# Cached attention: V in 2 KB rows, P times V as pairs of 64-row tiles, and a new order of the engines' work

## The chip, the cores and the metric

One core of a Trainium2 chip runs the whole kernel. The time is that of the device, in microseconds (us); medians of several runs are quoted. The engines are PE (matrix multiplies; PEld is its weight load), DVE (VectorE), ACT (ScalarE), POOL (GpSimd) and SP (SyncE, which only issues loads here). A run counts as slow when it is over 1.5% above the fastest run of the same kernel.

## The reference

Two independent blocks A and B, each a cached attention layer; bf16 throughout.

```python
# x (16, 64, 640), k_cache and v_cache (16, 32 heads, 512 keys, 128), wq (640, 4096), wo (4096, 640)
q = (x @ wq).reshape(B, Sq, H, Dh).transpose(0, 2, 1, 3)
scores = einsum("bhqd,bhkd->bhqk", q, k_cache) * Dh ** -0.5
p = softmax(scores, axis=-1)
o = einsum("bhqk,bhkd->bhqd", p, v_cache)
out = o.transpose(0, 2, 1, 3).reshape(B, Sq, H * Dh) @ wo
# result: concatenate([A, B], axis=-1)
```

K and V are 268 of the 292 MB that are read. Each pair of caches is used once.

## The kernel before

The work is cut into 128 packs: a pack is two batch elements and four heads. `build_plan` gives every operation a time in slots (a slot is about the time of one pack); sorting by it fixes each engine's order, and semaphores are derived from the reads and writes. SP's order of loads comes from deadlines. K and V have rings of five packs (buffers that are used in turn).

```python
AT = dict(..., QP=-1 + 0.40, QE=-1 + 0.58, KT=(-1 + 0.08, -1 + 0.70), S=0.0, ...
          TR=(0.95, 1.28), TE=(1.02, 1.38), PV=(1.20, 1.60), OE=(1.50, 1.72), OP=(1.70, 1.86), ...)

def em_LDV(e, op):                       # V: a head's 512 keys over 128 partitions, 4 keys = 1 KB each
    ...
    src = blocks[blk][2][2 * bp + b, 4 * j:4 * j + 4].rearrange("g (p t) d -> p g t d", p=128)
    ins = e.dma_start(v_ring[:, n % NV, b], src)

def em_S(e, op):                         # scores: 32 matmuls on 32-row, 64-column tiles
    ...
def em_TR(e, op):                        # 8 transposes for two heads; twice a pack
    ...
def em_PV(e, op):                        # P times V, twice a pack
    m = op.idx
    n, a = m // 2, m % 2
    for s in range(2):
        for b in range(2):
            for t in range(4):
                col = s * 128 + 64 * b
                last = e.matmul(o_ps[:, col:col + 64], v_ring[:, n % NV, b, 2 * a + s, t, :],
                                pT_ring[:, m % NT, s, t, 64 * b:64 * b + 64], start=(t == 0), stop=(t == 3))
...
def em_OP(e, op):                        # output projection: 512 + 128 columns a head
    ...
```

A matmul in the program is two PE instructions, LDWEIGHTS and MATMUL. So a pack costs PE 2 x (32 S + 16 transposes + 20 Q projection + 32 P times V + 8 output projection) = 216 instructions.

## Time and profile before

824.84 us, median of 3 runs (823.98 to 826.99).

| what | before |
|---|---|
| DMA | 376 GB/s in nearly every slice; 131,072 V packets of 1 KB, median 47 ns; 32,768 K packets of 4 KB, median 161 ns |
| PE, one pack without a stop | 5.31 us |
| PE, mean of packs 2 to 127 | 6.00 us |
| first pack after the start-up | 49.8 us; after the last S 18.6 us |

The first lines are the page's rows of 40 equal slices of the span: the busy share of PE and of the DMA engines in tenths, then GB/s.

```profile
PE   3069999999999999998778989999999999999994
...
DMA  9999999999999999999999999999999999999980
GB/s 329 364 372 367 377 378 376 378 373 379 373 374 376 371 380 375 373 375 370 339 319 377 372 378 377 376 376 376 376 375 373 377 373 376 375 374 376 377 284 13
```

Both PE and DMA look full. The next lines are the DMA queues: packets, MB, and the share of the 16 engines' span.

```profile
q1 hardware_dynamic: 193280, 292.06, 100.2%
q8 instruction: 112, 1.84, 0.9%
```

q1 carries the data (its packets overlap in time, hence over 100%). q8 carries instructions: 112 packets of 16,384 bytes for PE's 27,682 instructions, 1.84 MB, or 66 bytes each. PE's program is fetched block by block while the kernel runs, by the DMA engines that also bring K and V.

Now one pack on PE, in order of time: start, length, engine and line, operation, count.

```profile
331.10 1.14 PE L403 MATMUL ps<-kt_ring,qs_ring 32*64 32x512 bf16 x32
332.16 0.64 PE L462 MATMUL ps<-pT_ring,v_ring 128*128 128x64 bf16 x16
332.64 0.61 PE L446 MATMUL ps<-ident,pn_ring 128*128 128x128 bf16 x8
333.09 1.28 PE L380 MATMUL ps<-xT_ring,wqp_sb 128*128 128x128 bf16 x20
334.20 0.63 PE L462 MATMUL ps<-pT_ring,v_ring 128*128 128x64 bf16 x16
...
336.40 0.44 PE L403 MATMUL ps<-kt_ring,qs_ring 32*64 32x512 bf16 x8
```

S (L403) to S takes 336.40 - 331.10 = 5.30 us with no idle time between the groups (the left out lines are the output projection and the second transposes). (Lengths overlap: the profile models a matmul's end. Only starts are used here, so 332.16 to 332.64 is P times V.) Over the kernel the medians from each group's first weight load to the next group's are S 1.07, P times V 0.45 and 0.49, transposes 0.43 and 0.59, Q projection 1.12, output projection 1.17 us: some 5.31 us, which is called a pack without a stop below. But the mean pack takes 6.00. The group of P times V (busy us, mean ns | idle before it, releaser) and the table of waits (total us, times, longest) show what is between:

```profile
L462 PE MATMUL ps<-pT_ring,v_ring 128*128 128x64 bf16 x4096 | 168.6, 194 | 21.8 <-issue 11.4
```

```profile
PE ps L403 <- issue: 13.4, 21, 1.3
...
PE ps L462 <- issue: 11.4, 23, 1.9
...
PE ps L462 <- DMA v_ring<-in_B_v_cache_dram: 7.9, 11, 1.8
DVE kt_ring L393 <- DMA kn_ring<-in_A_k_cache_dram: 7.5, 1, 7.5
```

"issue" means that PE waited for nothing that the profile shows. Data is hardly ever late: 7.9 us on V, 7.5 us on K, once. SP instead waits for free K slots:

```profile
SPq L342 <- DVE kt_ring L393: 187.2, 123, 3.8
```

### The profile page before, as it was taken

To read this page: it belongs to the slowest core of one execution; us is meant where nothing else is said; L and a number is where in the kernel's file an instruction comes from. 1 tells how busy PE (TensorE), PEld (TensorE's weight loads), DVE (VectorE), ACT (ScalarE), POOL (GpSimd) and SP (SyncE) were. 2 spreads that over 40 slices of the span, in tenths; PEclk is the share of its full clock that TensorE was granted. 3 is DMA by queue.
4 is the path that set the end of the run, shared out by engine and by line. 5 is a ranking of instruction groups with operands and counts; after the bars stand their busy time and mean duration, and the time that the engine had idled before them with its cause. 6 is when DMAs were issued, how large, how long until landed. Compare 5 with 4: busy or idle time off the path is not lost.

```text
span 824.6 us, 31476 instructions
## 1 busy us (share of the span) xinstructions
PE 707.0 (86%) x13777; PEld 521.7 (63%) x13905; DVE 578.7 (70%) x902; ACT 419.6 (51%) x1313; POOL 388.2 (47%) x550
## 2 busy tenths in 40 slices
PE   3069999999999999998778989999999999999994
PEld 2046776767666767676556666666666666666773
DVE  3047787777777787777556767777777777787773
ACT  2025655555554645554444555555555464555552
POOL 2068444444444444445665444444454444454442
PEclk9999999999999999999999999999999999999997
DMA  9999999999999999999999999999999999999980
GB/s 329 364 372 367 377 378 376 378 373 379 373 374 376 371 380 375 373 375 370 339 319 377 372 378 377 376 376 376 376 375 373 377 373 376 375 374 376 377 284 13
DMA packets 195729, 296.79 MB, mean 360 GB/s; under 512 B 9216, under 2 KB 162816, under 8 KB 195584
## 3 DMA queue, kind: packets, MB, share of 16 engines
q1 hardware_dynamic: 193280, 292.06, 100.2%
q8 instruction: 112, 1.84, 0.9%
q10 hardware_dynamic: 2304, 2.62, 0.9%
q14 instruction: 33, 0.27, 0.1%
HBM read 292.03 MB, written 2.62 MB: 357 GB/s over the span
## 4 chain that ended last, share of the span: by engine, by line
PE 70%; DMA 10%; SPq 6%; issue 6%; POOL 5%; DVE 3%; ACT 0%; ACTq 0%
PE ps L380 15%; PE ps L403 14%; PE ps L462 14%; PE ps L446 12%; PE ps L476 9%; DMA v_ring<-in_B_v_cache_dram 8%; PE ps L479 5%; DMA ws_ring<-in_A_wq_dram 2%; SPq L349 2%; SPq L342 2%; DVE kt_ring L393 2%; POOL pn_ring L438 2%; POOL wqp_sb L356 1%; POOL wqp_sb L357 1%; SPq L335 1%
## 5 line engine op out<-in xcount | busy, mean ns | idle before, releaser
L438 POOL TENSOR_SCALAR pn_ring<-p_ring,recip 128x512 bf16<-128x512 bf16 x512 | 349.2, 694 | 382.0 <-DVE recip L433 382.0
L418 ACT ACTIVATE p_ring<-ps 128x512 bf16<-128x512 f32 x512 | 304.2, 597 | 262.2 <-PE ps L403 262.2
L393 DVE STREAM_TRANSPOSE kt_ring<-kn_ring 128x1024 f32<-128x1024 f32 x256 | 316.0, 1235 | 7.6 <-DMA kn_ring<-in_A_k_cache_dram 7.5
L451 DVE COPY pT_ring<-ps 128x1024 bf16<-128x1024 bf16 x256 | 177.1, 692 | 161.3 <-PE ps L446 161.3
L446 PE MATMUL ps<-ident,pn_ring 128*128 128x128 bf16 x2048 | 158.0, 220 | 48.0 <-POOL pn_ring L438 46.8
L462 PEld LDWEIGHTS ps<-pT_ring,v_ring 128*128 128x128 bf16 x4096 | 141.5, 98 | 80.1 <-issue 64.7
L462 PE MATMUL ps<-pT_ring,v_ring 128*128 128x64 bf16 x4096 | 168.6, 194 | 21.8 <-issue 11.4
L380 PE MATMUL ps<-xT_ring,wqp_sb 128*128 128x128 bf16 x2560 | 169.7, 222 | 11.4 <-issue 9.1
L403 PE MATMUL ps<-kt_ring,qs_ring 32*64 32x512 bf16 x4096 | 155.2, 398 | 15.5 <-issue 13.4
L446 PEld LDWEIGHTS ps<-ident,pn_ring 128*128 128x128 bf16 x2048 | 122.4, 98 | 64.3 <-POOL pn_ring L438 49.1
L380 PEld LDWEIGHTS ps<-xT_ring,wqp_sb 128*128 128x128 bf16 x2560 | 153.1, 114 | 14.7 <-issue 11.4
L468 ACT ACTIVATE oT_ring<-ps 128x256 bf16<-128x256 f32 x256 | 98.5, 385 | 117.6 <-PE ps L462 117.4
L476 PE MATMUL ps<-wo_sb,oT_ring 128*128 128x512 bf16 x384 | 132.9, 387 | 0.1
L386 DVE TENSOR_SCALAR qs_ring<-ps 128x512 bf16<-128x512 f32 x128 | 88.6, 692 | 60.7 <-PE ps L380 60.7
L479 PE MATMUL ps<-wo_sb,oT_ring 128*128 128x128 bf16 x512 | 113.0, 221 | 8.2 <-issue 1.7
L418 ACT ACTIVATION_READ_ACCUMULATOR p_ring<-ps 128x1 f32 x512 | 105.6, 206 | 0.0
L403 PEld LDWEIGHTS ps<-kt_ring,qs_ring 32*64 32x64 bf16 x4096 | 57.1, 104 | 63.1 <-issue 24.4
L476 PEld LDWEIGHTS ps<-wo_sb,oT_ring 128*128 128x128 bf16 x512 | 50.3, 98 | 65.6 <-ACT oT_ring L468 33.3
L479 PEld LDWEIGHTS ps<-wo_sb,oT_ring 128*128 128x128 bf16 x512 | 50.7, 99 | 0.2 <-issue 0.2
L433 DVE RECIPROCAL recip<-rowsum 128x2 f32<-128x2 f32 x256 | 36.3, 142 | 6.6 <-ACT p_ring L418 6.4
L356 POOL COPY wqp_sb<-ws_ring 128x1280 bf16<-128x1280 bf16 x16 | 20.0, 1253 | 41.4 <-DMA ws_ring<-in_A_wq_dram 41.4
L357 POOL COPY wqp_sb<-ws_ring 128x1280 bf16<-128x1280 bf16 x16 | 20.1, 1256 | 0.0
(19 smaller groups left out, 39.5 us busy)
## 6 DMA issues: line engine op xcount, KB each, us to landing
kn_ring<-in_A_k_cache_dram SPq DMA_DIRECT2D x128, 512.0 KB, 10.2
v_ring<-in_A_v_cache_dram SPq DMA_DIRECT2D x128, 512.0 KB, 10.7
kn_ring<-in_B_k_cache_dram SPq DMA_DIRECT2D x128, 512.0 KB, 10.2
v_ring<-in_B_v_cache_dram SPq DMA_DIRECT2D x128, 512.0 KB, 10.7
ws_ring<-in_A_wq_dram SPq DMA_DIRECT2D x8, 640.0 KB, 9.4
wo_sb<-in_A_wo_dram SPq DMA_DIRECT2D x8, 640.0 KB, 10.6
ws_ring<-in_B_wq_dram SPq DMA_DIRECT2D x8, 640.0 KB, 8.3
wo_sb<-in_B_wo_dram SPq DMA_DIRECT2D x8, 640.0 KB, 11.2
```

Source lines behind the costliest of these rows:

```text
L380: last = e.matmul(ps[:, 0, f * 128:(f + 1) * 128], w[:, kt, f, :], xT_ring[:, xs, kt, :], start=(kt == 0), stop=(kt == KT - 1))
L386: ins = e.tensor_scalar(qs_ring[:, op.idx % NQ].rearrange("p f b q -> p (f b q)"), ps[:, 0, :], scale, None, ALU.mult)
L393: ins = e.transpose(dst, kn_ring[:, n % NK, b, :].bitcast(F32))
L403: last = e.matmul(ps[64 * b:64 * b + 64, i, :], qs_ring[rows, n % NQ, f, b, :], kt_ring[rows, n % NKT, b, :, f // 2, :, f % 2], start=(f = ...
L418: ins = e.activation(dst, src, ACTF.Exp, scale=1.0, accum_out=rowsum[:, h:h + 1])
L438: ins = e.tensor_scalar(pn_ring[:, h % NPN, :], p_ring[:, h % NP, :], recip[:, (h // 2) % NR, h % 2:h % 2 + 1], 1.0, ALU.mult, ALU.mult)
L446: last = e.transpose(pt_ps[:, s, t, :], pn_ring[:, h % NPN, t * 128:(t + 1) * 128], ident[:, :])
L451: ins = e.tensor_copy(pT_ring[:, op.idx % NT].rearrange("p s t q -> p (s t q)"), pt_flat)
L462: last = e.matmul(o_ps[:, col:col + 64], v_ring[:, n % NV, b, 2 * a + s, t, :], pT_ring[:, m % NT, s, t, 64 * b:64 * b + 64], start=(t == ...
L468: ins = e.activation(oT_ring[:, op.idx % NO].rearrange("p s q -> p (s q)"), o_ps, ACTF.Copy)
L476: last = e.matmul(out_ps0, oT_ring[:, m % NO, s, :], wo_sb[:, h, 0:N0], start=(h == 0), stop=(h == H - 1))
L479: last = e.matmul(out_ps1, oT_ring[:, m % NO, s, :], wo_sb[:, h, N0:D], start=(h == 0), stop=(h == H - 1))
```

## The change

The intent: the DMA engines look saturated, and V's 1 KB rows cost more per byte than K's 4 KB rows. With 2 KB rows a head's 512 keys fill only 64 partitions, so two heads share the 128; P times V must then contract over 64 rows, in pairs of tiles. The two tiles of a pair write different banks of PSUM, the memory that PE writes its results to; one of these is shared with the last 128 output columns, which are therefore added up in SBUF by DVE once a pack (`OA`). P times V, its eviction and the output projection run once a pack instead of twice, and the order on all engines is new.

```diff
-    AT = dict(XT=-2 + 0.90, XE=-2 + 0.93, QP=-1 + 0.40, QE=-1 + 0.58, KT=(-1 + 0.08, -1 + 0.70), S=0.0,
-              ...
-              TR=(0.95, 1.28), TE=(1.02, 1.38), PV=(1.20, 1.60), OE=(1.50, 1.72), OP=(1.70, 1.86),
+    AT = dict(XT=-0.988, XE=-0.9, QP=-0.582, QE=-0.071, KT=(-0.704, -0.567), S=0.0,
+              ...
+              TR=(0.869, 1.222), TE=(1.062, 1.39), PV=1.623, OE=1.67, OP=2.225, OA=2.403,
 ...
-            src = blocks[blk][2][2 * bp + b, 4 * j:4 * j + 4].rearrange("g (p t) d -> p g t d", p=128)
+            src = blocks[blk][2][2 * bp + b, 4 * j:4 * j + 4].rearrange("(a s) (p t) d -> (s p) a (t d)", s=2, t=8)
 ...
-                    for t in range(4):
-                        col = s * 128 + 64 * b
-                        last = e.matmul(o_ps[:, col:col + 64], v_ring[:, n % NV, b, 2 * a + s, t, :],
-                                        pT_ring[:, m % NT, s, t, 64 * b:64 * b + 64], start=(t == 0), stop=(t == 3))
+                    for t in range(8):
+                        for s in range(2):
+                            rows = slice(64 * s, 64 * s + 64)
+                            col = a * 128 + 64 * b
+                            last = e.matmul(o_ps[:, s, col:col + 64], v_ring[rows, n % NV, b, a, t, :],
+                                            pT_ring[rows, (2 * n + a) % NT, t, 64 * b:64 * b + 64],
+                                            start=(t == 0), stop=(t == 7), tile_position=(64 * s, 0))
 ...
+        def em_OA(e, op):
+            j = op.idx % NJ
+            dst = out_sb[:, N0:D] if j == NJ - 1 else acc[:, :]
+            ins = e.tensor_copy(dst, out_ps1) if j == 0 else e.tensor_tensor(dst, acc[:, :], out_ps1, ALU.add)
 ...  (rings of P and P^T laid out by 64 keys and two heads; PSUM banks moved; a constant tile dropped)
```

P times V is now 64 matmuls a pack instead of 32: 280 PE instructions instead of 216.

## The prediction

> **What bounds the kernel now.** Two things nearly tie. The page's slice rows show the DMA engines busy in 9 tenths or more of every slice but the last two (376 GB/s). Yet compute hardly waits for data: the table of waits gives PE 7.9 us on V, VectorE 7.5 us on K. K lies landed 10 to 15 us before its transpose in the first half, 1.6 to 8.6 us in the second. In the steady state PE sets the pace. The timeline from 331.09 to 336.40 us is one pack with PE back to back: S 1.07, P times V 0.45 and 0.49, transposes 0.43 and 0.59, Q projection 1.11, output projection 1.17: 5.31 us. Packs average 5.9. The missing 0.6 us is holes in PE's stream that the waits call "issue". From 60 to 800 us I count 72 (75 us), nearly all ending 2.5 us after a 16 KB packet of the "instruction" queue (112 packets, 1.84 MB, for PE's 27,682 instructions: 66 B each). PE outruns its instruction fetch. Whole time: first real pack at 49 us, 126 packs at 6.0 us average (the block change costs some 15 us extra), 18 us of tail.
>
> **What the change does.**
> - DMA: V's 131,072 packets of 1 KB (median 46 ns, 4 KB ones 161 ns) become 65,536 of 2 KB; by the straight line between those, estimated 84 ns each instead of 92. Saves about 35 us of 16-engine time: some 785 us of DMA at full rate become 750. Off the steady critical path; it can remove at most the 15 us at the block change. The Trainium skill ("DMA: Bandwidth & Descriptors", Why small descriptors are slow) gives a fixed cost per packet; the trace agrees, about 8 ns.
> - PE: 32 P-times-V matmuls a pack (29 ns start to start) become 64 on 64 rows. The Trainium skill ("TensorE: Matmul & The Clock Gate", Part 3) says that matmuls on different row groups run concurrently; S does so in this trace. So I estimate 30 to 45 ns a pair: 1.0 to 1.4 us instead of 0.94. Two more changes of tiling mode, 0.1 us each (the breaks around S), add 0.2. PE without holes: estimated 5.5 to 5.9 us.
> - Fetch: 276 PE instructions a pack instead of 212, 64 of the new ones in the fastest stretch. With 2.5 us from fetch to use and about 75 instructions in hand (both from the trace), estimated holes grow from 0.6 to about 0.9 us a pack.
> - VectorE gains one 128x128 addition a pack (estimated 0.25 us on its 4.8). ScalarE's evictions shrink. Neither binds. P times V waits for that addition; Q projection covers it mostly.
> - Startup: PE still idles from 17 to 49 us behind the third Wq load, which the static order still puts after some 27 loads.
>
> **Time.** Pack estimated 6.2 to 6.9 us, mostly 6.5: 49 + 126 x 6.5 + 18 = 885 us. Range 825 to 945. Chances: faster by over 2% 0.10, within 2% 0.13, slower by over 2% 0.77.
>
> **What would show it.** Mean V packet near 84 ns, the queue's wait for K slots growing from 187 us; "instruction" packets near 144; PE holes over 100 us; P-times-V pair pitch 30 to 45 ns; K ready ever longer before use.
>
> **What would make it wrong.** Fetch holes that shrink once DMA is less loaded; a startup that the new order mends; pairs that don't overlap (pitch 60 ns: above 945 us); or DMA binding more than I think, which would give about 790 us.

(The counts in it, 212 and 276, leave out four instructions; they are 216 and 280. The same slip is in the expectations and names of the experiments below: 244 stands for 248, 228 for 232.)

## The result

893.87 us median of 4 runs (882.31 to 899.52), against 825.72 us for the kernel before. The ratio is 1.0745, with a 95% interval of 1.0639 to 1.0851. Ratios here are the mean time of one kernel's fast runs over that of the other's in the same rounds, so not quite the ratio of the medians. Two of the four runs count as slow by the 1.5% rule; the profiled one (span 894.0 us) is one of them, the fast ones are 882.31 and 891.87, and the granted clock does not tell them apart (0.977 and 0.984 in the slow ones, 0.981 and 0.988 in the fast). The reading below therefore leans on what the experiments show too.

The slices after:

```profile
PE   3078789888997897997978878888988989889885
...
DMA  9999989999998999899999998899998989989830
GB/s 341 378 379 390 374 320 362 335 319 376 326 368 311 364 382 344 314 367 303 331 385 389 391 396 317 288 361 312 362 346 267 388 299 367 338 302 360 311 124 13
```

DMA is no longer full (330 GB/s over the span, from 357), so the change has not made loads the limit. The queues:

```profile
q1 hardware_dynamic: 127744, 292.06, 90.2%
q8 instruction: 143, 2.34, 1.0%
```

The median V packet of 2 KB took 84 ns, as estimated, so the loads did become cheaper, though less than the two shares suggest: 90.2% of the longer span is 806 us of all 16 engines, 100.2% of the span before was 826. The instruction packets went from 112 to 143. PE's group of P times V (idle before it 33.2 us, from 21.8), PE's waits, and SP's wait for K slots:

```profile
L465 PE MATMUL ps<-pT_ring,v_ring 64*128 64x64 bf16 x8192 | 148.0, 191 | 33.2 <-issue 32.3
```

```profile
PE ps L465 <- issue: 32.3, 27, 3.8
...
PE ps L405 <- issue: 25.3, 21, 3.1
PE ps L447 <- issue: 18.4, 12, 2.5
...
PE ps L465 <- DVE acc L489: 0.7, 2, 0.4
```

```profile
SPq L344 <- DVE kt_ring L395: 413.9, 214, 5.8
```

The pairs themselves are fast. From the start of P times V to the next group it is 1.04 us for 64 matmuls, 16 ns from start to start where a full-array one took 29, so two run side by side. Before, the two halves took 0.94 us. A pack without a stop is now S 1.07, transposes 0.41, output projection 1.09, Q projection 1.26, P times V 1.04 and transposes 0.55, in this order: 5.42 us, only 0.11 more. The wait over the shared bank ("DVE acc") is 0.7 us in all. What grew are PE's waits on "issue", and SP waits twice as long for K slots because PE is behind. One such stop, in the same columns as the pack above:

```profile
304.03 0.90 PE L465 MATMUL ps<-pT_ring,v_ring 64*128 64x64 bf16 x50
305.80 0.38 PE L465 MATMUL ps<-pT_ring,v_ring 64*128 64x64 bf16 x14 [0.87 <-issue]
306.11 0.62 PE L447 MATMUL ps<-ident,pn_ring 128*128 128x128 bf16 x8
```

PE stops inside P times V, after 50 of 64 matmuls, for 0.87 us. Nothing in the program stands there, neither a semaphore nor a switch of shape. The longest:

```profile
673.75 1.07 PE L465 MATMUL ps<-pT_ring,v_ring 64*128 64x64 bf16 x61
678.57 0.28 PE L465 MATMUL ps<-pT_ring,v_ring 64*128 64x64 bf16 x3 [3.75 <-issue]
```

### What a hole is

I looked for stops of over 0.45 us, from the start of one PE instruction to the start of the next, that ended 1.1 to 1.9 us after an instruction packet had been transferred ("holes"), from 60 us to the last S. Before there are 50 of them, 45.9 us; after 81, 122.1 us. Counting PE's instructions in the trace, semaphore instructions included, they lie at one place in every 256. Most traces lack one matmul of a pack's output projection; with it put back, all 50 holes before lie at the same place, and after 78 of 81, the other three one instruction beside it. In experiment e1 below, whose trace lacks none, 94 of 96 do. 16,384 bytes are 256 instructions of 64 bytes. PE has run to the end of a block and the next is not there.

The Trainium skill ("Runtime: NRT & Kernel Launch", Instruction fetch mechanics) says that instructions come in 16 KiB blocks of 256, which this trace confirms, and that the cost of crossing a block is mostly hidden, which it does not: holes are 122.1 of 894.0 us.

The accounts of the 69.4 us between the two spans: holes +76.2 us; a pack without a stop +0.11 us, times 126 gives +13.9; other stops of over 0.45 us 29.6 before and 3.3 after (before, nearly all at the change of block A to B and in the 150 us after it, where loads were behind), -26.3. That sums to 63.8; the rest, some 6 us, lies in shorter stops, start-up and tail.

### The profile page after: what moved, and what is told of

It reads as the page before. It is cut to its first block, busy times and chain, and to the rows that moved or that the text cites. A ratio compares the mean times of both kernels' runs of the same rounds, so it can differ in the third digit from the quotient of the medians.

```text
span 894.0 us, 39557 instructions
## 1 busy us (share of the span) xinstructions
PE 732.5 (82%) x17873; PEld 541.9 (61%) x18001; DVE 602.4 (67%) x1030; ACT 405.1 (45%) x1185; POOL 386.8 (43%) x550
## 3 DMA queue, kind: packets, MB, share of 16 engines
q1 hardware_dynamic: 127744, 292.06, 90.2%
## 4 chain that ended last, share of the span: by engine, by line
PE 80%; issue 13%; SPq 3%; DMA 1%; ACT 1%; POOL 0%; DVE 0%; ACTq 0%
PE ps L405 17%; PE ps L382 16%; PE ps L447 16%; PE ps L465 15%; PE ps L481 10%; PE ps L483 6%; SPq L351 1%; SPq L344 1%; DMA ws_ring<-in_A_wq_dram 1%; ACT p_ring L420 1%; PE ps L365 1%; SPq L337 0%; POOL pn_ring L440 0%; POOL wqp_sb L358 0%; POOL wqp_sb L359 0%
## 5 line engine op out<-in xcount | busy, mean ns | idle before, releaser
L420 ACT ACTIVATE p_ring<-ps 128x512 bf16<-128x512 f32 x512 | 298.5, 598 | 211.5 <-PE ps L405 211.5
L447 PE MATMUL ps<-ident,pn_ring 128*128 128x128 bf16 x2048 | 164.3, 223 | 49.5 <-POOL pn_ring L440 29.8
L472 ACT ACTIVATE oT_ring<-ps 128x512 bf16<-128x512 f32 x128 | 76.4, 597 | 264.4 <-PE ps L465 264.4
L447 PEld LDWEIGHTS ps<-ident,pn_ring 128*128 128x128 bf16 x2048 | 118.9, 99 | 111.5 <-DVE pT_ring L453 39.8
L405 PE MATMUL ps<-kt_ring,qs_ring 32*64 32x512 bf16 x4096 | 159.2, 406 | 27.4 <-issue 25.3
L465 PE MATMUL ps<-pT_ring,v_ring 64*128 64x64 bf16 x8192 | 148.0, 191 | 33.2 <-issue 32.3
L465 PEld LDWEIGHTS ps<-pT_ring,v_ring 64*128 64x128 bf16 x8192 | 129.3, 95 | 48.5 <-issue 36.4
L481 PE MATMUL ps<-wo_sb,oT_ring 128*128 128x512 bf16 x384 | 123.0, 390 | 6.9 <-issue 6.9
L489 DVE TENSOR_TENSOR acc<-acc,ps 128x128 f32<-128x128 f32 x96 | 27.4, 285 | 29.8 <-PE ps L483 22.0
L358 POOL COPY wqp_sb<-ws_ring 128x1280 bf16<-128x1280 bf16 x16 | 20.0, 1251 | 42.5 <-DMA ws_ring<-in_A_wq_dram 42.5
```

The source lines that it names most:

```text
L405: last = e.matmul(ps[64 * b:64 * b + 64, i, :], qs_ring[rows, n % NQ, f, b, :], kt_ring[rows, n % NKT, b, :, f // 2, :, f % 2], start=(f = ...
L420: ins = e.activation(dst, src, ACTF.Exp, scale=1.0, accum_out=rowsum[:, h:h + 1])
L447: last = e.transpose(pt_ps[:, t, :], pn_ring[:, op.idx % NPN, t].rearrange("q s k -> q (s k)"), ident[:, :])
L465: last = e.matmul(o_ps[:, s, col:col + 64], v_ring[rows, n % NV, b, a, t, :], pT_ring[rows, (2 * n + a) % NT, t, 64 * b:64 * b + 64], star ...
L472: ins = e.activation(oT_ring[:, op.idx % NO].rearrange("p s a q -> p s (a q)"), o_ps, ACTF.Copy)
L481: last = e.matmul(out_ps0, oT, wo_sb[:, h, 0:N0], start=(h == 0), stop=(h == H - 1))
```

## The experiments

The theory: 64 more PE instructions a pack make PE reach the end of a fetched block sooner than the next one comes. Rivals: the new order or the chain over the shared bank costs the time; the 2 KB rows disturb something; the tiles are slow. The kernel before beside them had medians of 826.54 us (e1 to e4), 823.91 (e5 to e8), 824.98 (e9) and 825.28 (e10).

### e1: only the instructions, in the kernel before

```diff
-                    last = e.matmul(ps[:, 0, f * 128:(f + 1) * 128], w[:, kt, f, :], xT_ring[:, xs, kt, :], ...)
+    for hb in range(2):   # the 128 columns in two halves
+                    last = e.matmul(ps[:, 0, c0:c0 + 64], w[:, kt, f, :], xT_ring[:, xs, kt, 64*hb:64*hb + 64], ...)
-                last = e.matmul(out_ps0, oT_ring[:, m % NO, s, :], wo_sb[:, h, 0:N0], ...)
+    for q in range(4):    # the 512 columns in four quarters
+                last = e.matmul(out_ps0[:, c0:c0 + 128], oT_ring[:, m % NO, s, :], wo_sb[:, h, c0:c0 + 128], ...)
```

> The kernel before with 276 PE instructions a pack, as many as the changed kernel has, and the same columns streamed: the Q projection's 128-column matmuls cut in two of 64, the output projection's 512-column ones in four of 128. V rows, order, tiles and PSUM as before; the result is right. Fetch theory: holes after an instruction fetch grow from 0.6 to about 1.1 us a pack, some 138 fetches as in the changed kernel, total 870 to 895 us. Rival (order, shared bank or DMA rows cost the time): only the few ns of streaming more, 825 to 835 us.

933.52 us (928.49 to 939.06), ratio 1.1276, result correct. Nothing but the number and size of PE's instructions changed, and the kernel before became slower than the changed one. A pack without a stop rose from 5.31 to 5.54 us (that is 29 us of the 107), holes from 45.9 to 141.1 us. Slices, queue and waits:

```profile
DMA  9999899999899899997889999989999899899940
...
q8 instruction: 144, 2.36, 1.0%
```

```profile
PE ps L465 <- issue: 35.9, 25, 2.6
...
PE ps L481 <- issue: 25.9, 18, 2.4
```

I had expected 870 to 895: holes came to somewhat more per fetch than in the changed kernel (141.1 us over 139 fetches against 122.1 over 138), and the 64-column halves cost more streaming than I had allowed.

### e2: the changed kernel with half the instructions of P times V

```diff
-                for b in range(2):
-                    ... e.matmul(o_ps[:, s, col:col + 64], v_ring[rows, n % NV, b, a, t, :], pT_ring[..., 64 * b:64 * b + 64], ...)
+                    ... e.matmul(o_ps[:, s, a * 128:a * 128 + 128], v_ring[rows, n % NV, 0, a, t, :], pT_ring[rows, ..., t, :], ...)
```

> The changed kernel with half the P-times-V instructions: one 128-column matmul with one batch element's V in place of two 64-column ones (32 matmuls a pack instead of 64; result wrong on purpose). Columns streamed, tiling mode, order, DMA, PSUM as in the changed kernel. Fetch theory: holes fall from 1.0 to about 0.6 us a pack, 109 or so fetches, total 820 to 840 us. Rival (order, waits, DMA rows, bank): stays at 880 to 895 us.

783.04 us (782.37 to 783.48), ratio 0.9477. The result is wrong (both batch elements use the first one's V); loads, order, tiles, banks and streamed columns are those of the changed kernel, and a pack without a stop takes 5.37 us. Holes: 3.1 us. The slices' GB/s, the instruction queue, and PE's waits at P times V:

```profile
GB/s 331 385 376 383 393 398 397 398 397 399 397 396 399 379 398 391 392 397 396 353 383 387 388 391 398 396 398 396 396 395 393 395 395 393 396 391 393 397 342 28
...
q8 instruction: 111, 1.82, 1.0%
```

```profile
PE ps L463 <- DMA v_ring<-in_B_v_cache_dram: 6.3, 6, 1.8
...
PE ps L463 <- issue: 0.6, 2, 0.3
```

This was better than I had expected. Everything else in the change is good; the 64 extra instructions cost more than 100 us of its time (783.04 against 887.09, the mean of the changed kernel's fast runs). With them gone, DMA is full again, now at 395 GB/s.

### e3: the new order alone

V in 1 KB rows again and P times V as 32 full-array matmuls once a pack, in the changed kernel.

```diff
-            src = ....rearrange("(a s) (p t) d -> (s p) a (t d)", s=2, t=8)
+            src = ....rearrange("g (p t) d -> p g t d", p=128)
-                    for t in range(8):
-                        for s in range(2):  # 64-row tiles
+                    for s in range(2):
+                        for t in range(4):  # 128 rows; the rings of P laid out as before
```

> The changed kernel's order, rings, shared bank and extra VectorE addition, but V in 1 KB rows on 128 partitions and P times V as 32 full-array matmuls a pack (result right). Fetch theory: PE at 5.3 us and holes at 0.6 us a pack, total 815 to 835 us, like the kernel before. Rival (the order or the once-a-pack chain over the shared bank costs the time): 870 us or more.

817.93 us (817.32 to 818.71), ratio 0.9898, result correct. The order and the shared bank cost nothing; a pack without a stop is 5.20 us, holes fall to 23.4 us. Other stops are 43.1 us, one of them of 17.7 us at the block change. From pack 40 on, but for the block change, K lies ready only 1 to 2 us before use, so this kernel is bound by its loads:

```profile
GB/s 329 365 372 367 377 377 377 378 376 376 370 378 375 367 377 371 373 375 371 369 369 371 369 374 378 368 380 374 377 377 362 377 376 363 377 376 376 378 357 47
```

### e4: 2 KB rows alone

The kernel before with the other source pattern for V; V stands in the wrong places, so the result is wrong.

```diff
-            src = ....rearrange("g (p t) d -> p g t d", p=128)
-            ins = e.dma_start(v_ring[:, n % NV, b], src)
+            src = ....rearrange("(a s) (p t) d -> (s p) a (t d)", s=2, t=8)
+            ins = e.dma_start(v_ring[:, n % NV, b].rearrange("p (a e) t d -> p a (e t d)", a=2), src)
```

> The kernel before with V fetched in 2 KB rows and nothing else changed (V stands in the wrong places, result wrong on purpose). Theory (PE bounds the steady state, DMA only the block change): 810 to 825 us. Rival (DMA bounds the whole): 785 to 800 us. If 2 KB rows somehow slow the instruction fetch: above 835 us.

805.90 us (804.49 to 806.34), ratio 0.9747: 20.6 us, between the theory's 1 to 16 and the rival's 25 to 40, so a miss for both. Part is fewer holes (30.6 us against 45.9), part fewer other stops (22.6 against 29.6). So cheaper loads also help PE, which I had not foreseen.

### e5 and e6: the same two kernels with light loads

From the sixth pack on each K and V transfer carries a quarter of its bytes (results wrong). All engines' work stays.

```diff
-            ins = e.dma_start(kn_ring[:, n % NK, b, :], src)
+            w = 2048 if n < NK else 512
+            ins = e.dma_start(kn_ring[:, n % NK, b, 0:w], src[:, 0:w])     # V likewise
```

> The kernel before; from the sixth pack on each K and V transfer carries a quarter of its bytes (1 KB rows; result wrong on purpose). Work of all engines and PE's instructions as before. If the 2.5 us from fetch packet to use and the late fetches are PE's own affair: holes stay at about 0.6 us a pack, only the wait at the block change goes, 800 to 815 us. If instruction fetches come late because they queue behind the data in the DMA rings: holes nearly vanish, 735 to 760 us.

> The changed kernel with the same cut of the K and V bytes (result wrong on purpose). Own affair of PE: stays at 865 to 895 us. Queueing behind data: its PE needs 5.41 us a pack without holes, so 740 to 775 us.

765.61 us (763.21 to 766.28), ratio 0.9289, for the kernel before, and 764.00 us (761.72 to 764.45), ratio 0.9260, for the changed one (the first is 6 us above its range, the second inside). The holes are nearly gone: 4.5 and 7.5 us. The two of the kernel before do not lie at a block's end. The five of the changed one do, and all fall between 371 and 422 us, where the data rate rises from some 110 to 204 to 272 GB/s. Elsewhere PE runs through with 280 instructions a pack. Slices and queue of the changed kernel with light loads, and PE from a P times V on:

```profile
DMA  9996333333334444434679443333333334343300
...
q8 instruction: 143, 2.34, 1.3%
```

```profile
303.77 1.11 PE L467 MATMUL ps<-pT_ring,v_ring 64*128 64x64 bf16 x64
304.81 0.62 PE L449 MATMUL ps<-ident,pn_ring 128*128 128x128 bf16 x8
305.36 1.13 PE L407 MATMUL ps<-kt_ring,qs_ring 32*64 32x512 bf16 x32
```

So PE's instructions do not come late by themselves. They come late because the DMA engines are busy with data. From the moment at which PE executed the last instruction of one block, and so came to the next, to the start of the packet that brings the block after that, the median is 4.7 us in the kernel before and 1.0 us with light loads; in the changed kernel 3.8 and 0.7 us. From the packet's start to PE's next instruction after a hole it is 2.4 to 2.6 us in all kernels. The Trainium skill ("DMA: Bandwidth & Descriptors", Queues, rings and completion order) says that each engine takes turns between its queues, a whole packet at a time, and that such a packet is typically some 9 to 17 descriptors. If a descriptor is what the profile calls a packet, a single row (no run here shows it), one turn of 4 KB rows at 161 ns each is an estimated 1.4 to 2.7 us, from that page's count and this trace's time. So waiting for turns may be a good part of the delay of 4 us, but it is not shown.

### e7: an earlier start of PE

```diff
-    t_now = -8.0
+    t_now = -4.0        # in e3: SP's plan starts later in its own time, so the third Wq load comes sooner
```

> The changed kernel's order with V in 1 KB rows (818 us in the earlier run), and the DMA queue's static plan started later in its own time (-4 slots instead of -8), so that the third Wq load comes after some 11 loads instead of 27 and PE's first idle stretch (17 to 49 us) ends sooner. If DMA bounds that kernel from end to end: 808 to 818 us, little gain. If the late start of PE still counts: 790 to 803 us. Result right.

817.59 us (816.81 to 817.93), ratio 0.9916, result correct. The first pack after the start-up comes at 27.2 us instead of 49.8, and the end does not move. That kernel is bound by its loads from end to end, as e3 said; PE's idle stretch at the start is free.

### e8: a dose between

Wide matmuls as in e2, for one of the two head pairs only: 248 instructions a pack; result wrong.

> The changed kernel with the wide P-times-V matmuls for one of the two head pairs of a pack only: 244 PE instructions a pack, between 212 (783 us) and 276 (890 us); result wrong on purpose. Fetch theory, cost growing with the instructions: 825 to 850 us. If instead the cost comes only past a threshold near 276: 785 to 805 us.

826.81 us (824.17 to 831.55), ratio 1.0018; holes 77.5 us. Between 783 and 894 and at the lower end of what was expected: the cost grows with the count and is not a threshold at 280.

### e9: fewer loads under way

If the fetch queues behind the loads under way, fewer of them should help. A load now also waits until the one four (or three) before it has landed; results are right.

```diff
-            for op in progs[eng]:
+            for i, op in enumerate(progs[eng]):
                 waits = list(op.waits)
+                if eng == "sp" and i >= 4:
+                    old = progs[eng][i - 4]
+                    waits.append((old.sem, old.count))
```

> The changed kernel, complete and right, with one more wait in the load queue: a load is issued only when the load four before it has landed, so at most four are under way (before: issue to landing 10 us at 1.35 us a load, some seven under way). Queueing theory: an instruction fetch then starts 1 to 2.5 us after its block boundary instead of 3.8, holes fall below 0.3 us a pack, DMA stays full; 775 to 805 us. Rival (the fetch is slowed by the sharing of the engines at full rate, not by the depth of the queue): 870 us or more.

> The same with at most three loads under way (about 4 us of data[...]). Queueing theory: fetches start sooner still, but the DMA engines may run dry between loads; 775 to 815 us. Rival: 870 us or more.

> The kernel before with at most four loads under way (right). Queueing theory: its holes (0.6 us a pack) go too, and what is left is DMA with 1 KB rows: 805 to 820 us. Rival: unchanged at 825 us, or slower if four are too few to keep the engines full.

Misses in time, all three. They were run on another chip. The changed kernel with four: 868.80 us (863.53 to 868.96), ratio 1.0520, some 18 us less than its fast runs without (887.09), but far from 805. There the limit changes little: SP waits for free slots anyway, and the median time from issue to landing only fell from 6.5-7.1 us to 5.8-5.9. The median fetch starts 3.98 us after the crossing, against 3.83 without the limit; the delays only vary less (eight in ten lie between 2.5 and 5.1 us, against 1.0 and 5.8), and holes are 100.8 us instead of 122.1. With three: 1013.53 us (1011.09 to 1016.08), ratio 1.2290; the engines run dry (293 GB/s) and PE waits for data, with a delay of 2.9 us and holes of 40.0 us.

The kernel before with four: 868.17 us (865.37 to 872.77), ratio 1.0521, slower than without, at 341 GB/s over the span instead of 360. Here the limit does change the queue: from issue to landing the median fell from 10.2-10.7 us to 6, the fetch's delay from 4.7 to 2.6 us, and the holes from 45.9 to 8.7 us, of which only 0.5 us lie at a block's end. So the holes went, as the queueing theory had said, but PE now waits for V:

```profile
PE ps L462 <- DMA v_ring<-in_B_v_cache_dram: 44.8, 41, 2.4
...
PE ps L462 <- DMA v_ring<-in_A_v_cache_dram: 28.5, 22, 2.3
```

The loads under way are thus part of the delay in the kernel before (or the lower data rate that came with fewer of them; the runs do not separate the two). They do not explain the delay of the changed kernel, and a limit that takes the holes away costs more in data than it gains.

### e10: a trade between the two limits

In e3, every fourth pack gets 2 KB rows and tiled pairs (232 instructions a pack on average).

```diff
+            if n % 4 == 0:
+                ...  # V "(a s) (p t) d -> (s p) a (t d)", 64-row pairs
+            else:
+                ...  # V "g (p t) d -> p g t d", full array
```

A first build, which is not on record, was refused before it ran, for a race: a pack of one layout overwrote P while the half of another layout was still read. One more dependency, which the recorded edit has, mended it.

> A trade between the two limits: the changed kernel's order; every fourth pack has V in 2 KB rows and P times V in pairs of 64-row tiles, the other three have 1 KB rows and full-array matmuls (result right). DMA falls by a quarter of the 2 KB rows' gain (from the 818 us of the all-1-KB kernel by some 9 us); PE instructions are 228 a pack on average, between 212 (hardly a hole) and 244 (827 us). If both limits move as the runs suggest: 800 to 812 us, faster than both kernels. If the pack with 276 instructions pays its holes in full: 818 to 830 us.

821.26 us (818.80 to 823.73), ratio 0.9964, result correct. It was run on another chip. It missed the 800 to 812 us that I hoped for and fell in the range of holes paid in full: loads got cheaper (380 GB/s in many slices), but holes rose to 63.0 us from 23.4.

The best right version stays e3 (or e7): about 1% faster than the kernel before, and 8% faster than the changed one.

### One rule over the runs

Let a block's time be 256 instructions at the pace of a pack without a stop, and the fetch's time be its median delay after the crossing plus the time from its packet to PE's next instruction (2.4 to 2.6 us). The fetch is late by the difference.

| kernel | instructions a pack | block, us | fetch, us | late by | holes per fetch, us | time, us |
|---|---|---|---|---|---|---|
| e5 before, light loads | 216 | 6.29 | 3.5 | -2.8 | 0.04 | 765.61 |
| e6 changed, light loads | 280 | 4.95 | 3.3 | -1.7 | 0.05 | 764.00 |
| e9 before, four under way | 216 | 6.29 | 5.1 | -1.2 | 0.08 | 868.17 |
| e2 changed, wide | 216 | 6.37 | 6.4 | 0.0 | 0.03 | 783.04 |
| e9 changed, three under way | 280 | 4.95 | 5.4 | 0.4 | 0.29 | 1013.53 |
| e3 order alone | 216 | 6.17 | 6.6 | 0.5 | 0.22 | 817.93 |
| e4 2 KB rows alone | 216 | 6.29 | 6.8 | 0.5 | 0.29 | 805.90 |
| before | 216 | 6.29 | 7.2 | 0.9 | 0.43 | 824.84 |
| e8 | 248 | 5.57 | 6.9 | 1.3 | 0.64 | 826.81 |
| changed | 280 | 4.95 | 6.3 | 1.3 | 0.88 | 893.87 |
| e9 changed, four under way | 280 | 4.95 | 6.3 | 1.4 | 0.73 | 868.80 |
| e1 before, more instructions | 280 | 5.06 | 6.9 | 1.8 | 1.01 | 933.52 |

The block's time is 256 / instructions x the pack without a stop (for example 256 / 216 x 5.31 = 6.29); holes per fetch are the holes' total over the fetches of the same stretch. Where hardly any hole follows a fetch (e5 and the kernel before with four under way), 2.5 us stand for the second part of the fetch's time. e7 and e10 are left out: the one is e3 but for its start, the other mixes two kinds of pack. The rule works with medians and leaves out the spread, so it does not compute the holes and does not order kernels whose fetches are late by nearly the same, but it separates the groups. Where the fetch is not late, holes are below 0.1 us a fetch; half a microsecond late, 0.2 to 0.3; 1.3 to 1.8 us late, 0.6 to 1.0. It describes the traces that it was drawn from and has not been tried on another kernel. The time is not set by holes alone: with three loads under way, or four in the kernel before, PE also waits for data.

## Why the prediction was right

Predicted 885 us in a range of 825 to 945; measured 893.87. Point by point:

- "In the steady state PE sets the pace": right for the kernel before. With data lying ready, SP waited for K slots. Yet the margin was thin: e3 shows that with a slightly faster PE (5.20 us) the same 1 KB loads bind at 818 us.
- "PE outruns its instruction fetch": right, shown by e1 (instructions added, nothing else: +107 us) and e2 (instructions taken away: 783 us). One number was wrong: of the 72 stops and 75 us that I put down to it, only 50 and 45.9 us follow a fetch; the rest are at the block change and in the 150 us after it. The growth that I expected per pack (0.6 to 0.9) was then too small: it was 0.36 to 0.97 us (45.9 and 122.1 us over 126 packs).
- "30 to 45 ns a pair" held at its low end: 64 matmuls took 1.04 us, about 32 ns a pair. "5.5 to 5.9 us" without holes was too pessimistic: the pack took 5.42 us. The Trainium skill ("TensorE: Matmul & The Clock Gate", Part 3) says that matmuls in different row groups run at the same time, and the trace agrees. The new order gave back 0.11 us (e3: 5.20 against 5.31), and the tiles with two more changes of tiling mode cost 0.22 (5.42 against 5.20). A pack without a stop that was set too long and a growth of the holes that was set too small nearly cancelled: pack 6.57 measured, 6.5 predicted. That the number came so close is therefore partly luck; the cause and the direction were right.
- DMA: 84 ns a packet right. "It can remove at most the 15 us at the block change" was too low: e4 shows 20.6 us, because cheaper loads also shorten the holes.
- The start-up and the tail (48.2 and 18.1 us) were right; the wait for K slots grew to 413.9 us, instruction packets were 143 (144 said), K lay ready 22 to 28 us before use through most of the run.
- The warning "fetch holes that shrink once DMA is less loaded" names the mechanism that e5 and e6 found. I had taken the 2.5 us after the packet for the whole latency; the larger part is before the packet, 3.8 to 4.7 us, and the load on the engines sets it. Nor were the "75 instructions in hand" a fixed reserve: at the packet's start PE had a median of 97 left in its block before, 78 after and over 200 with light loads. Less load on DMA did not rescue the change, since at 330 GB/s the delay had fallen by less than 1 us while a block's time had fallen by 1.3 us.

What stays open: why the delay is 4 us at full load, since four loads under way cut it to 2.6 us in the kernel before but left it at 3.98 us in the changed one (e9); and why it is 4.7 us with the old order, 4.1 with the new one at the same rows (before and e3).

## What to carry to other kernels

Count an engine's instructions as a cost of their own: where loads keep the DMA engines full, each block of 256 PE instructions has to last longer than its fetch takes (here 6 to 7 us), or PE stops. A change that makes loads cheaper by cutting matmuls into more pieces can lose more by the pieces than it gains; before adopting it, add the pieces alone to the old kernel and see. Stops under "issue" in the middle of a group, at equal distances in instructions, are the sign to look for.

## What the Trainium skill lacked or had wrong

- "Runtime: NRT & Kernel Launch", Instruction fetch mechanics: the cost of crossing a 16 KiB boundary is not mostly hidden beside saturated loads. Holes were 45.9 us of 824.6 in the kernel before, 122.1 us of 894.0 in the changed one, 141.1 us of 937.3 in e1, and 7.5 us of 762.1 with light loads.
- No page that I read has the latency of that fetch: 0.7 to 1.0 us (light loads) or 3.8 to 4.7 us (full) from the end of the block before to the packet's start, then some 1.0 us for the packet and 1.4 us more until PE goes on.
- "DMA: Bandwidth & Descriptors", Queues, rings and completion order: it does not say how many rows of a load issued from SP make one packet, that is how long another queue waits for its turn. A row took 0.05 to 0.16 us here and the fetch waited 3.8 to 4.7 us at full load; which wait that is, the runs leave open.
- "DMA: Bandwidth & Descriptors", Bandwidth: no table of packet times by size for loads issued from SP. Here medians at full load were 46 to 47 ns for 1 KB, 84 to 85 for 2 KB and 159 to 161 for 4 KB, about 9 ns plus 38 ns per KB.
- "TensorEngine Tiling (Array Packing)", Performance Considerations: a fixed cost of each matmul is there, but nothing on what the added instructions do to the instruction fetch. Pairs of 64-row tiles took little longer than full-array matmuls (1.04 against 0.94 us a pack) and lost by their count (holes 122.1 us against 3.1 in e2).
